# Attention over a key and value cache on one core: keys of five more pieces by plain loads and PE transposes

## The chip, the core and the metric

One core of a Trainium2 chip runs the whole program in one launch. The metric is device time in microseconds (us), the median of several executions. The engines are named as in the profile: PE (TensorE, matmuls and transposes), ACT (ScalarE), DVE (VectorE), POOL (GpSimd) and SP (SyncE, which here only issues DMAs). Each engine runs its own instructions in the order in which they are written and waits on semaphores for the others.

## The reference

```
B, Sq, D = 8, 112, 640;  H, Sk, Dh = 32, 512, 192
q = (x @ wq).reshape(B, Sq, H, Dh).transpose(0, 2, 1, 3)
scores = einsum("bhqd,bhkd->bhqk", q, k_cache) * Dh ** -0.5
p = softmax(scores)
o = einsum("bhqk,bhkd->bhqd", p, v_cache)
return o.transpose(0, 2, 1, 3).reshape(B, Sq, H * Dh) @ wo
```

All inputs and the output are bf16. The caches are 50 MB each; x is 1.1 MB, wq and wo are 7.9 MB each.

## The kernel before

**Tiles.** The 32 heads are cut into NR = 4 rounds of HU = 8 heads. A piece is one round of one batch element: 8 heads x 512 keys x 192 numbers, 1.57 MB of keys and as much of values; there are 32 pieces, in order of round, then batch. A step is half a piece (4 heads): step n belongs to piece n // 2, and there are 64 of them, S0 to S63. A group g is a round and half of the batch (4 elements), 8 in all.

**Work of PE.** `("X", c)` transposes rows of x (5 transposes). `("Q", g, lp, c)` makes 128 columns of q for a pair of heads and a group: 5 matmuls of 128x448 (line 566); ACT moves the result to `qr` (line 571). `("S", n)` makes the scores of a step: 8 full matmuls (lines 611 and 613) and 8 over 64 rows, two side by side in the two row halves of PE (lines 624 and 626). DVE then takes the minimum of the negated scores and copies them (`smax`, line 639), ACT does the exponential (line 644), DVE the reciprocal of the sum and the normalization (line 648). `("PT", n)` turns the probabilities on PE with 32 transposes over 64 or 48 rows, side by side in the two row halves (line 682); DVE and ACT move them out (line 695). `("PVt", n)` and `("PVm", n)` multiply with values (lines 715 and 726); ACT moves the result (line 736). `("O", g, m, part)` is half of a block of the output projection, 6 matmuls of 128x448 (line 748; 224 columns in group 7), which DVE adds to `accT` (lines 762 and 763). `("OF", b)` turns the output, and a DMA stores it.

**Keys.** The scores need keys with the 192 numbers of a head on partitions. For pieces 2 to 31 `load_k` (line 130) has the DMA engines transpose on the way in (`dma_start_transpose`, line 136) into one of KS = 4 buffers of `kt`. For pieces 0 and 1 (NPL = 2) `load_kn` (line 165) brings keys as they lie into a staging place `kn`: the third value buffer `vt[:, 2]` for piece 0, and wo's region for piece 1. `("K", i, u, bank, engine)` then turns one head on PE, 6 transposes of 128x128 (line 541) into one PSUM bank, and ACT or DVE moves 128x768 numbers to `kt` (line 547).

**Order.** Nothing is scheduled at run time. Four lists, ORDER_PE, ORDER_ACT, ORDER_DVE and ORDER_SP (lines 193, 270, 352 and 487), give each engine's order; a program made them beforehand. `Plan.run` emits the waits from the dependencies that each entry names. Banks 0 to 3 of PSUM hold scores; the other entries get a bank number in the list, mostly 4 to 7, and wait until that bank's last user has been moved out (`fill`, line 870).

**Loads.** All loads and stores are issued by SP, in the order of ORDER_SP; an entry that waits holds back all behind it. `("KN", i, lo, n)` are the plain key loads, `("K", i)` the transposing ones, `("V", i)` values (3 buffers, so V(i) waits for the use of V(i-3)), `("WQ", r, lp, n)` pieces of wq (round r, pairs of heads lp on; it waits for the last Q fills that read the round before), `("WO", r)` wo of a round, `("TD", n)` probabilities of five late steps, which a DMA turns in place of PE, and `("OUT", b)` stores. A Q fill of group g is moved out to one of 8 slots, so that it waits for the last score of group g-2 that read the slot.

Of the kernel before, what the change touches and what calls it, by code (L numbers as in the profile page):

```python
# [7 lines left out]
ACTF = mybir.ActivationFunctionType  # L8
# [44 lines left out]
def build_mha_kernel(nc, x, k_cache, v_cache, wq, wo, out):  # L53
    B, SQ, D = x.shape
# [3 lines left out]
    HU = 8  # L58
# [9 lines left out]
    NPL = 2  # L68
# [17 lines left out]
    with ExitStack() as es:  # L86
# [26 lines left out]
        kn = [vt[:, VS - 1], wo_flat[:, 0:HU * 768].rearrange("p (u c) -> p u c", u=HU)]  # L113
# [28 lines left out]
        def load_v(i):  # L142
            r, b = divmod(i, B)

            def emit(e):
                src = v_cache[b, r * HU:(r + 1) * HU].rearrange("u (r q) d -> r u (q d)", q=4)
                return e.dma_start(vt[:, i % VS], src)
            deps = [("PVm", 2 * (i - VS) + j, 1) for j in range(2)] if i >= VS else []
            if i == VS - 1:
                deps = [("KT", 0, u) for u in range(HU)]  # L150
            add("SP", ("V", i), deps, emit, f"mV{i % VS}", 16)
# [13 lines left out]
        def load_kn(i, lo, hi):  # L165

            def emit(e):
                return e.dma_start(kn[i][:, lo:hi, :], k_cache[i, lo:hi].rearrange("u (r q) d -> r u (q d)", q=4))
            add("SP", ("KN", i, lo, hi - lo), [], emit, f"mKN{i}_{lo}", 16)
            kn_of.update({(i, u): ("KN", i, lo, hi - lo) for u in range(lo, hi)})  # L170
# [14 lines left out]
        def load_wo(r):  # L185
# [4 lines left out]
            old = [("O", 2 * r - 1, m, 1) for m in range(DC)] if r else [("KT", 1, u) for u in range(HU)]  # L190
# [3 lines left out]
            ("X", 0, 7, "ACT"), ("X", 1, 4, "DVE"), ("K", 0, 0, 0, "DVE"), ("K", 0, 1, 2, "ACT"), ("X", 3, 3, "DVE"),  # L194
            ("X", 2, 0, "DVE"), ("K", 0, 2, 5, "ACT"), ("K", 0, 3, 6, "ACT"), ("Q", 0, 0, 1, 4), ("Q", 0, 1, 1, 0),
            ("Q", 0, 0, 2, 1), ("Q", 0, 1, 2, 3), ("Q", 0, 1, 0, 1), ("K", 0, 6, 4, "ACT"), ("Q", 0, 0, 0, 7),
            ("Q", 0, 3, 2, 2), ("S", 0), ("Q", 0, 3, 0, 6), ("Q", 0, 3, 1, 7), ("Q", 0, 2, 2, 5), ("Q", 0, 2, 0, 3),
            ("Q", 0, 2, 1, 1), ("K", 1, 3, 2, "DVE"), ("K", 0, 5, 7, "DVE"), ("K", 0, 7, 4, "ACT"),
            ("K", 1, 1, 6, "DVE"), ("K", 0, 4, 2, "DVE"), ("X", 4, 5, "ACT"), ("K", 1, 2, 7, "ACT"),
            ("X", 5, 2, "ACT"), ("X", 6, 4, "ACT"), ("K", 1, 5, 1, "DVE"), ("K", 1, 0, 3, "DVE"),  # L200
            ("K", 1, 4, 5, "ACT"), ("S", 1), ("Q", 1, 0, 1, 5), ("K", 1, 7, 6, "DVE"), ("Q", 1, 0, 2, 4),
            ("K", 1, 6, 7, "ACT"), ("S", 2), ("PT", 0, 5), ("Q", 1, 2, 0, 4), ("Q", 1, 0, 0, 7), ("Q", 1, 1, 0, 5),
            ("Q", 1, 1, 1, 7), ("Q", 1, 3, 0, 4), ("S", 3), ("PT", 1, 5), ("Q", 1, 1, 2, 7), ("PVt", 0, 4),
            ("PVt", 1, 6), ("PVm", 0), ("PVm", 1), ("S", 4), ("PT", 2, 4), ("Q", 1, 3, 2, 1), ("Q", 1, 3, 1, 7),
            ("S", 5), ("PT", 3, 5), ("PVt", 2, 4), ("PVm", 2), ("S", 6), ("PVt", 3, 4), ("PT", 4, 6), ("PVm", 3),
            ("S", 7), ("Q", 1, 2, 1, 7), ("PT", 5, 4), ("PVt", 4, 6), ("PVm", 4), ("Q", 1, 2, 2, 1), ("PT", 6, 5),
            ("S", 8), ("PVt", 5, 5), ("PVm", 5), ("Q", 2, 0, 1, 4), ("Q", 2, 0, 2, 1), ("Q", 2, 0, 0, 7), ("S", 9),
            ("PT", 7, 6), ("PVt", 6, 0), ("PVm", 6), ("Q", 2, 2, 1, 5), ("S", 10), ("PVt", 7, 4), ("Q", 2, 1, 0, 7),
            ("PVm", 7), ("PT", 8, 6), ("Q", 2, 2, 2, 4), ("S", 11), ("PT", 9, 4), ("Q", 2, 1, 1, 6), ("S", 12),
            ("PVt", 8, 4), ("PVt", 9, 6), ("PVm", 9), ("PVm", 8), ("Q", 2, 1, 2, 0), ("PT", 10, 4), ("Q", 2, 3, 2, 1),  # L210
            ("O", 0, 1, 0, 6), ("O", 0, 0, 0, 7), ("O", 0, 0, 1, 7), ("O", 0, 1, 1, 6), ("S", 13), ("PT", 11, 4),
            ("Q", 2, 2, 0, 7), ("Q", 2, 3, 1, 1), ("PVt", 10, 4), ("PVt", 11, 6), ("PVm", 11), ("PVm", 10),
            ("O", 0, 4, 0, 6), ("S", 14), ("PT", 12, 4), ("Q", 3, 0, 1, 7), ("O", 0, 2, 0, 4), ("Q", 2, 3, 0, 5),
            ("O", 0, 4, 1, 6), ("S", 15), ("PT", 13, 5), ("O", 0, 2, 1, 4), ("O", 0, 3, 0, 5), ("O", 0, 3, 1, 5),
            ("S", 16), ("PVt", 12, 6), ("PVm", 12), ("PT", 14, 4), ("PVt", 13, 0), ("PVm", 13), ("Q", 3, 1, 0, 7),
            ("Q", 3, 0, 2, 6), ("PT", 15, 4), ("S", 17), ("PVt", 14, 5), ("PVm", 14), ("Q", 3, 2, 0, 1),
            ("PVt", 15, 4), ("PVm", 15), ("S", 18), ("PT", 16, 4), ("Q", 3, 0, 0, 7), ("O", 1, 0, 0, 6), ("S", 19),
# [12 lines left out]
            ("PVt", 27, 5), ("PT", 28, 0), ("PVm", 27), ("O", 2, 2, 0, 4), ("O", 2, 2, 1, 4), ("Q", 4, 3, 0, 7),  # L230
            ("S", 31), ("PT", 29, 5), ("Q", 5, 0, 0, 4), ("O", 2, 3, 0, 6), ("O", 2, 3, 1, 6), ("S", 32),
            ("PVt", 28, 4), ("PVt", 29, 6), ("PVm", 28), ("PVm", 29), ("PT", 30, 0), ("O", 2, 4, 0, 7),
            ("O", 2, 4, 1, 7), ("S", 33), ("PT", 31, 6), ("Q", 5, 0, 2, 5), ("Q", 5, 1, 0, 4), ("Q", 5, 0, 1, 5),
            ("S", 34), ("PVt", 30, 6), ("PVt", 31, 4), ("PVm", 30), ("PVm", 31), ("PT", 32, 6), ("O", 3, 0, 0, 1),
            ("O", 3, 0, 1, 1), ("PT", 33, 4), ("S", 35), ("PVt", 32, 4), ("PVt", 33, 6), ("PVm", 33), ("PVm", 32),
            ("S", 36), ("O", 3, 2, 0, 7), ("PT", 34, 4), ("O", 3, 1, 0, 6), ("Q", 5, 1, 1, 0), ("Q", 5, 1, 2, 3),
            ("O", 3, 1, 1, 6), ("S", 37), ("Q", 5, 2, 0, 6), ("O", 3, 3, 0, 4), ("O", 3, 2, 1, 7), ("PT", 35, 5),
            ("O", 3, 3, 1, 4), ("S", 38), ("PVt", 34, 6), ("PVm", 34), ("Q", 5, 2, 1, 5), ("Q", 5, 3, 2, 0),
            ("PT", 36, 4), ("PVt", 35, 6), ("Q", 5, 2, 2, 0), ("Q", 5, 3, 0, 1), ("PVm", 35), ("Q", 5, 3, 1, 4),
            ("S", 39), ("PT", 37, 5), ("O", 3, 4, 0, 4), ("O", 3, 4, 1, 4), ("PVt", 36, 6), ("PVm", 36), ("S", 40),  # L240
            ("PT", 38, 5), ("Q", 6, 1, 0, 7), ("Q", 6, 0, 0, 0), ("Q", 6, 0, 2, 1), ("PVt", 37, 3), ("PVm", 37),
# [771 lines left out]
```

## Time and profile before

| what | us |
|---|---|
| median of 3 runs (448.17 to 450.05) | 448.45 |
| the profiled execution, its own time | 448.98 |
| span of its instructions | 447.0 |
| ACT, exponentials (line 644), 256 x 715 ns | 182.6 |
| DVE, minimum and copy of scores (line 639), 256 x 684 ns | 169.8 |
| PE, Q fills (line 566), 480 x 353 ns | 101.9 |
| PE, output projection (line 748), 480 x 341 ns | 93.5 |

The page gives busy time of each engine and its share of the span, the span in 40 slices with one digit each (9 stands for 90% or more), and groups of instructions. Matmuls are pipelined: the 353 ns of one Q matmul overlap the next, which starts about 190 ns after it, so that counts are priced by the distance of starts and not by the mean duration. A wait is shown as the engine's idle time before an instruction and what ended it.

### The profile page before, as it was taken

The page shows a single profiled execution, that of the slowest core. Times are in us where ns is not written, and L with a number is a line of the kernel's source. Part 1 is how long each engine was busy: PE and PEld are TensorE (multiplying, and loading weights), DVE is VectorE, ACT ScalarE, POOL GpSimd, SP SyncE. Part 2 cuts the span into 40 slices and gives each one's busy share as a digit, 9 for nine tenths or more (in the row PEclk, how much of TensorE's full clock was granted, in tenths as well). Part 3 has the DMA queues.
Part 4 walks back from the last instruction along what each step waited for, and adds up shares of the span by engine and source line. Part 5 has one row for each costly group of instructions (what it writes and reads, how often), then busy time and mean ns, then how long its engine had stood idle before and what let it go on. Part 6 is the DMA issues. An engine that isn't in the chain of part 4 may idle for free.

```text
span 447.0 us, 14859 instructions
## 1 busy us (share of the span) xinstructions
PE 423.9 (95%) x6229; PEld 295.9 (66%) x6229; DVE 353.5 (79%) x1142; ACT 332.9 (74%) x753; POOL 0.7 (0%) x6
## 2 busy tenths in 40 slices
PE   8999788999999999999999999999999999999996
PEld 5566555666666666776676666666676757665886
DVE  1368897876989877888898877898789968899862
ACT  2689888885768778797679748788668676974784
POOL 0000000000000000000000000000000000000000
PEclk9999999999999999999999999999999999999999
DMA  8999999999999999999999999999999999999782
GB/s 273 373 349 201 211 239 325 364 314 240 251 303 223 244 351 366 231 325 307 210 321 292 240 251 254 360 328 246 321 240 245 236 268 367 301 204 235 212 225 64
DMA packets 247858, 121.93 MB, mean 273 GB/s; under 512 B 195440, under 2 KB 247792, under 8 KB 247792
## 3 DMA queue, kind: packets, MB, share of 16 engines
q1 hardware_dynamic: 247792, 120.99, 109.8%
q8 instruction: 49, 0.80, 0.8%
q14 instruction: 17, 0.14, 0.1%
HBM read 70.35 MB, written 1.15 MB: 160 GB/s over the span
## 4 chain that ended last, share of the span: by engine, by line
PE 70%; DVE 15%; ACT 7%; DMA 3%; issue 3%; SPq 0%; DVEq 0%; ACTq 0%
PE ps L566 17%; PE ps L748 15%; DVE s_sb L639 9%; PE ps L726 8%; PE ps L624 6%; PE ps L611 6%; PE ps L613 5%; PE ps L715 5%; PE ps L682 5%; ACT p_sb L644 3%; DVE p_sb L648 2%; DVE pT_sb L695 2%; DMA wq_sb<-in_wq_dram 2%; DMA wq_sb<-p_sb 2%; ACT oT_sb L736 1%
## 5 line engine op out<-in xcount | busy, mean ns | idle before, releaser
L644 ACT ACTIVATE p_sb<-s_sb,nmx 112x512 bf16<-112x512 f32 x256 | 182.6, 715 | 46.6 <-DVE s_sb L639 30.8
L639 DVE TENSOR_SCALAR_CACHE_REDUCE s_sb<-ps 112x512 f32<-112x512 f32 x256 | 169.8, 684 | 36.7 <-PE ps L626 18.8
L566 PE MATMUL ps<-xT_sb,wq_sb 128*128 128x448 bf16 x480 | 101.9, 353 | 4.0 <-DVE s_sb L639 2.5
L748 PE MATMUL ps<-oT_sb,wo_sb 128*128 128x448 bf16 (+1 forms) x480 | 93.5, 341 | 0.4 <-ACT qr L571 0.4
L648 DVE TENSOR_SCALAR p_sb<-p_sb,rinv 112x512 bf16<-112x512 bf16 x256 | 80.3, 347 | 1.3
L566 PEld LDWEIGHTS ps<-xT_sb,wq_sb 128*128 128x128 bf16 x480 | 42.8, 98 | 43.4 <-DVE s_sb L639 4.2
L748 PEld LDWEIGHTS ps<-oT_sb,wo_sb 128*128 128x128 bf16 x480 | 44.0, 98 | 36.7 <-ACT pT_sb L695 0.9
L736 ACT ACTIVATE oT_sb<-ps 128x672 bf16<-128x672 f32 x64 | 45.8, 724 | 25.6 <-PE ps L726 25.1
L571 ACT ACTIVATE qr<-ps 128x448 bf16<-128x448 f32 x96 | 49.7, 536 | 19.0 <-PE ps L566 18.5
L695 ACT ACTIVATE pT_sb<-ps 128x768 bf16<-128x768 bf16 x59 | 47.2, 800 | 11.5 <-PE ps L682 10.5
L726 PE MATMUL ps<-pT_sb,vt 128*128 128x112 bf16 x944 | 54.5, 213 | 0.0
L726 PEld LDWEIGHTS ps<-pT_sb,vt 128*128 128x128 bf16 x944 | 47.5, 98 | 4.0
L644 ACT ACTIVATION_READ_ACCUMULATOR p_sb<-s_sb,nmx 112x1 f32 x256 | 48.8, 191 | 0.0
L695 DVE COPY pT_sb<-ps 128x1024 bf16<-128x1024 bf16 x59 | 40.4, 685 | 6.7 <-PE ps L682 5.7
L682 PEld LDWEIGHTS ps<-ident,p_sb 64*128 64x128 bf16 (+1 forms) x1888 | 32.3, 94 | 15.4 <-DVE p_sb L648 6.6
L682 PE MATMUL ps<-ident,p_sb 64*128 64x64 bf16 (+1 forms) x1888 | 37.6, 185 | 4.5 <-DVE p_sb L648 1.2
L611 PE MATMUL ps<-kt,qr 128*112 128x256 bf16 x128 | 36.2, 283 | 3.8 <-DVE s_sb L639 2.2
L715 PE MATMUL ps<-pT_sb,vt 128*64 128x112 bf16 x944 | 32.5, 215 | 4.6 <-ACT pT_sb L695 2.6
L715 PEld LDWEIGHTS ps<-pT_sb,vt 128*64 128x64 bf16 x944 | 25.4, 109 | 15.1 <-ACT pT_sb L695 4.8
L613 PE MATMUL ps<-kt,qh 128*112 128x256 bf16 x128 | 34.9, 273 | 0.0
L613 PE MATMUL ps<-kt,qr 128*112 128x256 bf16 x128 | 34.9, 273 | 0.0
L611 PE MATMUL ps<-kt,qh 128*112 128x256 bf16 x128 | 34.9, 273 | 0.0
(60 smaller groups left out, 451.3 us busy)
## 6 DMA issues: line engine op xcount, KB each, us to landing
vt<-in_v_cache_dram SPq DMA_DIRECT2D x32, 1536.0 KB, 10.2
wo_sb<-in_wo_dram SPq DMA_DIRECT2D x4, 1920.0 KB, 13.6
wq_sb<-in_wq_dram SPq DMA_DIRECT2D x14, 480.0 KB, 7.3
vt<-in_k_cache_dram SPq DMA_DIRECT2D x2, 768.0 KB, 7.4
wo_sb<-in_k_cache_dram SPq DMA_DIRECT2D x1, 1536.0 KB, 12.7
out_dram<-xT_sb SPq DMA_DIRECT2D x8, 140.0 KB, 3.1
wq_sb<-in_wq_dram SPq DMA_DIRECT2D x1, 960.0 KB, 10.3
kt<-in_x_dram SPq DMA_DIRECT2D x2, 320.0 KB, 4.5
```

What stands on the lines that cost most here:

```text
L566: mm = e.matmul(ps[:, bank, 0:SG], wq_sb[:, dc, c0:c0 + 128], xT_sb[:, dc, bh * SG:(bh + 1) * SG], start=(dc == 0), stop=(dc == DC - 1))
L611: e.matmul(ps[0:SQ, 2 * j, hs], ev, ktb[:, :, 0, cs(i)], start=(h == 0), stop=False, skip_group_check=True)
L613: mm = e.matmul(ps[0:SQ, 2 * j + 1, hs], od, ktb[:, :, 2, cs(i)], start=(h == 0), stop=False, skip_group_check=True)
L639: return e.tensor_scalar(s_sb[:, a, :].rearrange("p (e c) -> p e c", e=2), ps[0:SQ, 2 * j:2 * j + 2, h * 256:(h + 1) * 256], -scale, None, ...
L644: return e.activation(p_sb[:, k, :], s_sb[:, a, :], ACTF.Exp, bias=nmx[:, k:k + 1], scale=-1.0, accum_out=rsum[:, k:k + 1])
L648: return e.tensor_scalar(p_sb[:, k, :], p_sb[:, k, :], rinv[:, k:k + 1], None, op0=ALU.mult)
L682: ends.append(e.transpose(psb[:, bank + t, i * w:(i + 1) * w], p_sb[lo:hi, (4 * n + k) % 8, q * 128:(q + 1) * 128], ident[lo:hi, lo:hi]))
L695: return e.activation(dst, src, ACTF.Copy) if j == 0 else e.tensor_copy(dst, src)
L715: mm = e.matmul(ps[64 * h:64 * h + 64, b0 + j, SQ:2 * SQ], vtb[:, h0 + 2 * j + h, d0:d0 + 64], pT(j, h, q), start=(q == 0), stop=(q == 3))
L726: mm = e.matmul(ps[:, b0 + j, 2 * h * SQ:(2 * h + 1) * SQ], vtb[:, h0 + 2 * j + h, d0:d0 + 128], pT(j, h, q), start=(q == 0), stop=(q == 3))
L736: return e.activation(dst.rearrange("p (j c) s -> p j c s", j=2), ps[:, b0:b0 + 2, 0:3 * SQ].rearrange("p j (c s) -> p j c s", c=3), ACTF. ...
L748: mm = e.matmul(ps[:, bank_of["O", g, m, 0], 0:nc_], wo_sb[:, k, m * 128:(m + 1) * 128], oT_sb[:, g % 2, k, 0:nc_], start=(k == 0), stop=( ...
```

## The change

Keys of pieces 2 to 6 no longer come by transposing DMAs. NPL goes from 2 to 7: their keys are loaded as they lie, into staging places that alternate between wo's region (pieces 1, 3, 5) and a part of `accT`'s region behind that of x (pieces 2, 4, 6). A load of keys waits until the piece two before it has been turned; the first load of wo waits until pieces 1, 3 and 5 are turned; the first sums into `accT` wait for pieces 2, 4 and 6.

The turning of keys, now for 7 pieces, is done for two heads at a time: 12 pairs of transposes over 64 rows, one in each row half of PE, into two PSUM banks, and two moves of 128x768 numbers, each on ACT or DVE. From piece 4 on a move also waits until the scores that last read the `kt` buffer are done. Before there were 16 entries of one head with one move each (8 on ACT, 8 on DVE); now there are 28 entries of two heads with two moves each (25 on ACT, 31 on DVE). All four lists are new, over the whole length of the kernel.

```diff
-    NPL = 2
+    NPL = 7
...
-        kn = [vt[:, VS - 1], wo_flat[:, 0:HU * 768].rearrange("p (u c) -> p u c", u=HU)]
+        kn = [vt[:, VS - 1]]
+        for i in range(1, NPL):
+            flat = wo_flat[:, 0:HU * 768] if i % 2 else acc_flat[:, 3 * D:3 * D + HU * 768]
+            kn.append(flat.rearrange("p (u c) -> p u c", u=HU))
...
-                deps = [("KT", 0, u) for u in range(HU)]
+                deps = [("KT", 0, p) for p in range(LP)]
...
-            add("SP", ("KN", i, lo, hi - lo), [], emit, f"mKN{i}_{lo}", 16)
+            old = [("KT", i - 2, p) for p in range(lo // 2, hi // 2)] if i > 2 else []
+            add("SP", ("KN", i, lo, hi - lo), old, emit, f"mKN{i}_{lo}", 16)
...
-            old = [("O", 2 * r - 1, m, 1) for m in range(DC)] if r else [("KT", 1, u) for u in range(HU)]
+            old = [("O", 2 * r - 1, m, 1) for m in range(DC)] if r else [("KT", i, p) for i in range(1, NPL, 2) for p in range(LP)]
...
-        def k_transposes(i, u, bank, eng):
-            def emit(e):
-                for c in range(6):
-                    mm = e.transpose(psb[:, bank, c * 128:(c + 1) * 128], kn[i][:, u, c * 128:(c + 1) * 128], ident[:, :])
-                return mm
...
-            add("PE", ("KT", i, u), [kn_of[i, u]], emit)
-            add(eng, ("evK", i, u), [("KT", i, u)], evac)
+        def k_transposes(i, p, bank, engs):
+            def emit(e):
+                for x in range(12):
+                    c, u = divmod(x, 2)
+                    ends = [e.transpose(psb[:, bank + t, x * 64:(x + 1) * 64],
+                                        kn[i][64 * t:64 * t + 64, 2 * p + u, c * 128:(c + 1) * 128],
+                                        ident[64 * t:64 * t + 64, 64 * t:64 * t + 64]) for t in range(2)]
+                return tuple(ends)
+
+            add("PE", ("KT", i, p), [kn_of[i, 2 * p], kn_of[i, 2 * p + 1]], emit, ("PE", "PE2"))
+            old = [("St", 2 * (i - KS) + 1, 3)] if i >= KS else [("XT", x) for x in range(4)] if i == KS - 1 else []
+            for t in range(2):
+                def evac(e, t=t):
+                    dst = kt[:, i % KS].rearrange("p a m (u t s) -> p (a m) u t s", t=2, s=64)[:, :, 2 * p:2 * p + 2, t, :]
+                    src = psb[:, bank + t, 0:768].rearrange("p (c u s) -> p c u s", c=6, u=2)
+                    return e.activation(dst, src, ACTF.Copy) if engs[t] == "ACT" else e.tensor_copy(dst, src)
+                add(engs[t], ("evK", i, p, t), [("KT", i, p)] + old, evac)
...
-                    ([("evK", n // 2, 4 * qd + i) for i in range(4)] if n // 2 < NPL else [("K", n // 2)]), emit)
+                    ([("evK", n // 2, 2 * qd + i, t) for i in range(2) for t in range(2)] if n // 2 < NPL else [("K", n // 2)]), emit)
...
-            deps = [("O", g, m, 1)] + ([("oacc", g - 2, m)] if r else [("XT", c) for c in range(4, B * SQ // 128)])
+            deps = [("O", g, m, 1)] + ([("oacc", g - 2, m)] if r else
+                                         [("XT", c) for c in range(4, B * SQ // 128)] +
+                                         [("KT", i, p) for i in range(2, NPL, 2) for p in range(LP)])
```

SP's list, its first part before and after:

```diff
-            ("X", 0), ("KN", 0, 0, 4), ("X", 1), ("WQ", 0, 0, 1), ("WQ", 0, 1, 1), ("KN", 0, 4, 4), ("WQ", 0, 2, 2),
-            ("KN", 1, 0, 8), ("X", 2), ("V", 0), ("V", 1), ("V", 2), ("K", 2), ("K", 3), ("K", 4), ("K", 5), ("K", 6),
-            ("WQ", 1, 0, 1), ("WQ", 1, 2, 1), ("V", 3), ("WQ", 1, 1, 1), ("V", 5), ("V", 4), ("WQ", 1, 3, 1),
-            ("WO", 0), ("V", 6), ("K", 7), ("K", 9), ("K", 8), ("V", 7), ("V", 8), ("K", 11), ("K", 10), ("K", 12),
+            ("X", 0), ("X", 1), ("WQ", 0, 1, 1), ("WQ", 0, 0, 1), ("KN", 0, 0, 4), ("X", 2), ("WQ", 0, 2, 2),
+            ("KN", 0, 4, 4), ("KN", 1, 0, 8), ("KN", 2, 0, 8), ("V", 2), ("V", 0), ("WQ", 1, 0, 1), ("KN", 3, 0, 8),
+            ("KN", 4, 0, 8), ("V", 1), ("V", 3), ("WQ", 1, 2, 1), ("WQ", 1, 1, 1), ("KN", 5, 0, 8), ("WQ", 1, 3, 1),
+            ("KN", 6, 0, 8), ("V", 4), ("K", 7), ("K", 8), ("WO", 0), ("V", 6), ("V", 5), ("V", 7), ("K", 10),
```

PE's list from S5 to S13, after (K has the piece, the pair of heads, the bank and the two engines):

```
("S", 5), ("K", 3, 1, 6, "ACT", "DVE"), ("PT", 3, 4), ("PVt", 2, 6), ("K", 3, 2, 4, "ACT", "DVE"), ("PVm", 2),
("S", 6), ("K", 4, 1, 4, ...), ("K", 4, 2, 6, ...), ("K", 4, 0, 4, ...), ("K", 4, 3, 0, ...), ("Q", 2, 1, 0, 7),
("PT", 4, 4), ("Q", 2, 0, 0, 6), ("PVt", 3, 0), ("PVm", 3), ("K", 5, 1, 5, ...), ("S", 7), ("PT", 5, 4), ("PVt", 4, 6),
("PVm", 4), ("Q", 2, 0, 2, 5), ("S", 8), ("K", 5, 3, 4, ...), ("PT", 6, 6), ("Q", 2, 0, 1, 5), ("K", 5, 0, 0, ...),
("Q", 2, 2, 1, 4), ("K", 5, 2, 6, ...), ("S", 9), ("PVt", 5, 4), ("PVm", 5), ("K", 6, 2, 6, ...), ("PT", 7, 0),
("Q", 2, 2, 2, 6), ("Q", 2, 1, 1, 7), ("S", 10), ("PVt", 6, 6), ("PVm", 6), ("K", 6, 0, 4, ...), ("K", 6, 3, 0, ...),
("PT", 8, 6), ("Q", 2, 3, 1, 1), ("Q", 2, 2, 0, 0), ("PVt", 7, 5), ("PVm", 7), ("Q", 2, 3, 0, 1), ("K", 6, 1, 4, ...),
("PT", 9, 6), ("S", 11), ("PVt", 8, 4), ("PVt", 9, 6), ("PVm", 9), ("PVm", 8), ("S", 12), ("PT", 10, 5),
("O", 0, 0, 0, 4), ("Q", 2, 1, 2, 6), ("Q", 2, 3, 2, 7), ("O", 0, 0, 1, 4), ("S", 13)
```

## The prediction

> **What bounds the kernel now.** I read the totals and slices of the page first, then the busy time stage by stage, then SP's queue, and last the rows that price the parts of the change. A stage here runs from the first score matmul of one step to that of another (S0 starts at 17.3 us, S5 at 51.7, S9 at 75.5, S13 at 101.8, S63 at 427.8, read from the timeline's L611 rows).
>
> ```profile
> span 447.0 us, 14859 instructions
> ...
> PE 423.9 (95%) x6229; PEld 295.9 (66%) x6229; DVE 353.5 (79%) x1142; ACT 332.9 (74%) x753; POOL 0.7 (0%) x6
> ...
> DMA  8999999999999999999999999999999999999782
> GB/s 273 373 349 201 211 239 325 364 314 240 251 303 223 244 351 366 231 325 307 210 321 292 240 251 254 360 328 246 321 240 245 236 268 367 301 204 235 212 225 64
> ```
>
> Two resources are near full: PE at 95% and the DMA queue, whose slices stay at nine tenths until about 402 us. The GB/s row tells the two kinds of transfer apart: 349 to 373 in the early slices, where plain loads run, 201 and 211 in the fourth and fifth, where keys come by DMA transposes.
>
> ```profile
> core 0: us, PE busy (x) PEld busy (x) DVE busy (x) ACT busy (x) POOL busy (x), PEclk, DMA share, GB/s
> 17.30:51.70 34.40, 31.91 (x397) 21.79 (x397) 25.68 (x82) 28.50 (x65) 0.00 (x0) 1.00 1.20 266
> 51.70:75.50 23.80, 19.77 (x346) 13.91 (x347) 21.06 (x71) 19.51 (x46) 0.00 (x0) 1.00 1.18 275
> 75.50:101.80 26.30, 24.56 (x375) 16.92 (x375) 20.97 (x69) 21.63 (x51) 0.00 (x0) 1.00 1.11 338
> 101.80:427.80 326.00, 318.23 (x4692) 220.60 (x4691) 274.66 (x888) 244.83 (x561) 0.00 (x0) 1.00 1.14 274
> 427.80:447.00 19.20, 14.76 (x325) 13.46 (x321) 8.39 (x28) 10.81 (x21) 0.00 (x0) 0.99 0.45 142
> ```
>
> From S13 to S63 PE is busy 97.6% of the time. From S0 to S13 it is 76.2 of 84.5 us (90%); the worst part is S5 to S9, where DVE (21.1 of 23.8) leads and PE idles 4.0 us. The granted clock is 1.00 nearly throughout and plays no part.
>
> ```profile
> 25.88 41.57 SPq L136 DMA_TRANSPOSE kt<-in_k_cache_dram  x5
> 67.50 1.14 SPq L179 DMA_DIRECT2D wq_sb<-in_wq_dram  x2
> 68.69 0.53 SPq L147 DMA_DIRECT2D vt<-in_v_cache_dram  x1
> ```
>
> SP's timeline shows why fillers are missing there: the transposes of pieces 2 to 6 hold SP from 25.9 to 67.5 us, and wq of round 1 is issued only then. Its first piece lands 4.8 us after issue (the view of line 179 in that window), at 72.3; the first Q of group 2 starts at 72.5. V of piece 3 lands 9.3 us after issue, at 78.0, and is used at 78.4.
>
> **The change, part by part.**
>
> ```profile
> 26.66 1.17 PE L541 MATMUL ps<-ident,wo_sb 128*128 128x128 bf16 x18
> ...
> 34.48 0.52 PEld L682 LDWEIGHTS ps<-ident,p_sb 64*128 64x128 bf16 x32
> ```
> ```profile
> PEld ps L624 <- issue: 11.4, 64, 0.2
> ```
> ```profile
> L547 ACT ACTIVATE kt<-ps 128x768 bf16<-128x768 bf16 x8 | 6.3, 806 | 0.0
> L547 DVE COPY kt<-ps 128x768 bf16<-128x768 bf16 x8 | 4.2, 552 | 8.8 <-PE ps L541 8.8
> ```
>
> *PE, key transposes.* Old form: 18 matmuls in 1.17 us less the last one's tail, 56 ns apart, so 0.335 us a head, 16 heads: 5.4 us. The new form (64-row matmuls in two row halves) is that of the probability transposes: 32 loads in 0.52 us, less the last one's 0.09, is 15 further pairs in 0.43: 29 ns a pair. A pair of heads has 12 pairs of matmuls: 0.35 us; 28 pairs of heads: 9.7 us. Net +4.4 us.
>
> *PE, changes of tiling.* At 64 of 64 steps PE's loads wait 0.18 us on "issue" where the 128-row score matmuls hand over to the 64-row ones; start to start this is 0.20 us instead of the 0.11 inside a run, so a change costs 0.095 us. Counting changes between full, 64-row and 64-column matmuls in the two lists: 45 against 64 up to S13 (+1.8 us), 216 against 190 behind it (-2.5 us). In all PE's work grows by 3.7 us.
>
> *PE, work moved.* Up to S13 the new list holds three more Q fills (5 matmuls, 0.95 us each) and two fewer O halves (1.14 us each): with keys and changes of tiling +6.7 us there. From S13 to S63 the Q and O come back (-0.5 us), the changes give -2.5, and four O halves of group 7 (0.575 us each) go behind S63: -5.3, and -5.0 when every entry is summed at its own rows. Behind S63: +2.0.
>
> *ACT and DVE.* The key evacuations grow from 8 to 25 on ACT and 8 to 31 on DVE, all ahead of S13. Back to back one takes 0.70 us on ACT (chain: 1.41 for two), 0.47 on DVE: +11.9 and +10.8 us.
>
> *DMA and SP.* The last four of the five transposes leave SP 27.6 us apart in sum, 6.9 each; a plain 1.57 MB at the 366 GB/s of 17 to 33 us takes 4.3. Five make the queue 13 us lighter, and wq of round 1 moves from behind the transposes to among the key loads. I credit no gain for this by itself: it shows only as a better filled PE, below. The Trainium skill, Advanced Engine Details and Errata, X-Bar Transpose (TRN2), says transposing DMAs are as fast as plain ones; 6.9 against 4.3 us here says otherwise. By that rule the queue would not get lighter and the faster rival below would lose its support; the sum would stay.
>
> *New waits on SP, which issues in order.* wq of lane pair 0, round 1, waits for Q(1,0,*), which come after S1; behind it queue the keys of 3 and 4 and V of 1, used from S3 on. Keys of 5 wait for piece 3's last turn (after S5) and hold wq(1,3), keys of 6, V4 and K7. PE has 7.6 us of listed work before it wants them; alone they need 4.3 us plus 2 (an output's landing), under load 12.7 (keys of piece 1): 0 to 5 us late, I take 0 since only two 480 KB pieces are ahead. wo now waits for pieces 1, 3 and 5 and stands behind K8, which waits for S9: about 7 us of issue and 15.6 to land (wo's first load, before) against 21.6 us until its first use: 0 to 2 us late, I take 0. Both ends stay in the range.
>
> *Sum.* Stage loads of after are those of the stage table plus what the two lists add, at these prices and those of the timeline's rows. S5 to S9, as an example: ACT 19.5 + 10 key evacuations x 0.70, one evacuation of Q and one of PV fewer and one of probabilities more (-0.4) = 26.1; PE 19.8 + 10 x 0.35 + 0.4 for changes of tiling - 1.2 for one PV fewer = 22.5; DVE 21.1 + 10 x 0.47 - 0.67 for one copy of q fewer = 25.1. S0 to S5 likewise: PE 33.3, ACT 31.6, DVE 28.7. S9 to S13: PE 26.2, ACT 24.0, DVE 23.2. The busiest engine's loads add to 33.3 + 26.1 + 26.2 = 85.6; before, they add to 31.9 + 21.1 + 24.6 = 77.6 in 84.5 us, 92%. With less waiting for loads the share should rise, but three engines with nearly equal loads that hand over to each other will not reach the 97.6% that PE reaches alone later. I take the middle, 94.8%: 90.3 us, +5.8 (bounds +1.1 at 100%, +8.5 at 92%, +12.1 if ACT's additions hide nowhere). S0 itself: by the lists PE has 1.0 us more ahead of it, and x and wq come with 0.79 MB of keys fewer ahead of them, 2.1 us at 366 GB/s: I take 0 (-1 to +1). S13 to S63: -5.0 if PE sets the pace, 0 if the hand-over between DVE and ACT does; PE is the busiest by far (318 against 275), so -4.0. Behind S63: PE idles 4.4 of 19.2 us and part of the 2.0 falls there: +0.7 (0 to +2). Sum: +5.8 - 4.0 + 0.7 = +2.5 us. The profiled execution took 448.98 us for a span of 447.0, 0.5 above the median 448.45; from that median: **451.0 us**.
>
> **Rivals.**
> *The lighter queue pays (faster).* The slack of 0.2 and 0.4 us at wq and V3 says that loads set the pace from S5 to S12. If all of the early idle time was theirs, the early stage runs at its busiest engine's load (+1.1), the later one at PE's (-5.1), and the tail hides: -4.0, 444.4 us. For it: PE idles 4.0 us just where wq is late. Against it: DVE leads there, and DVE and ACT get the most new work. It decides once the early stage grows by less than 2 us.
> *Evacuation becomes the bound (slower).* ACT's 12.1 us come on top: +12.1 - 4.0 + 0.7 = +8.8, 457.3 us. For it: S5 to S9 makes ACT the busiest (26.1), with work that exps wait behind. Against it: ACT idled 18% of S0 to S13. The Trainium skill, TensorEngine Tiling (Array Packing), PSUM Bottleneck, has it that tiling speeds TensorE but not the emptying of PSUM; the trace agrees in kind, 0.35 us to turn a pair of heads against 0.70 + 0.47 to empty it.
> *The halves don't run side by side.* Then a pair of heads takes 24 x 29 ns = 0.70 us, +9.8 us of PE: 460.8 us at most. The probability transposes speak against it.
>
> **How the numbers follow.** Forecast 0.41 (its own range 447 to 455, four parts in ten of it under 450.7), faster rival 0.31, evacuation 0.20, not side by side 0.08. A measurement here can't tell less than 0.5% (446.2 to 450.7) from no change. Faster by more: the rival but for its upper edge, 0.28. Within: that edge and 0.17 of the forecast, 0.20. Slower by more: the rest of the forecast and the last two, 0.52. The range leaves one in ten on each side: 443.5 to 457.5.
>
> **What would show it.** S13 at about 107.6 us (102.9 for the faster rival, 113.9 for evacuation); ACT busier than PE between S5 and S9; 0.35 us for a pair of heads at the new transposes; S13 to S63 in about 322 us; no wait of Q on wq and none of O on wo. A first O that waits for wo, or turns of pieces 5 and 6 that wait for their loads, would make the forecast wrong upwards; PE over 95% busy from S5 to S9 would make it wrong downwards.

## The result, and the profile after

The changed kernel takes 445.86 us (median of 19 runs, 443.96 to 448.78), the kernel before 448.37 (19 runs, 447.41 to 451.85) on the same chip: ratio 0.9938, 95% interval 0.9919 to 0.9958. It is 0.6% faster, where 2.5 us slower had been forecast. Medians, here and below, are over all runs of a kernel, but ratios and their intervals leave out runs more than 1.5% above that kernel's fastest. The profiled execution of the changed kernel took 446.26 us for a span of 444.4.

First the page after: span, busy time of PE, DVE and ACT, and four rows of the 40 slices.

```profile
span 444.4 us, 16108 instructions
...
PE 425.1 (96%) x6805; PEld 304.5 (69%) x6805; DVE 363.2 (82%) x1165; ACT 344.4 (78%) x770; POOL 0.7 (0%) x6
...
PEclk9999999999999999999999999999999999989999
DMA  8999999998999999999999999999999999999952
GB/s 278 373 337 323 347 299 285 226 342 276 232 289 317 215 270 270 365 247 288 238 223 324 301 236 267 360 370 234 234 266 313 256 267 371 234 173 242 237 176 80
```

The fourth and fifth slices move 323 and 347 GB/s where before they moved 201 and 211: plain loads run there now. PEclk has one 8 near the end, of which more below. Now the busy time stage by stage; the cuts are the starts of S0, S5, S9, S13, S25, S41, S55 and S63 in this trace.

```profile
core 0: us, PE busy (x) PEld busy (x) DVE busy (x) ACT busy (x) POOL busy (x), PEclk, DMA share, GB/s
17.50:52.80 35.30, 33.23 (x609) 22.63 (x609) 29.00 (x88) 31.79 (x69) 0.00 (x0) 1.00 1.00 345
52.80:77.40 24.60, 22.70 (x555) 16.80 (x553) 23.56 (x75) 24.44 (x52) 0.00 (x0) 1.00 1.03 292
77.40:106.90 29.50, 26.64 (x500) 19.11 (x497) 24.39 (x81) 26.06 (x59) 0.00 (x0) 1.00 1.12 305
106.90:184.50 77.60, 77.60 (x1155) 54.32 (x1154) 66.52 (x210) 58.04 (x135) 0.00 (x0) 1.00 1.13 266
184.50:284.20 99.70, 98.29 (x1512) 69.77 (x1511) 87.80 (x288) 80.25 (x185) 0.00 (x0) 1.00 1.17 277
284.20:372.80 88.60, 88.13 (x1332) 61.76 (x1331) 75.24 (x245) 68.23 (x155) 0.00 (x0) 1.00 1.15 288
372.80:423.10 50.30, 47.92 (x673) 35.82 (x672) 43.28 (x143) 37.14 (x87) 0.00 (x0) 0.97 1.06 236
423.10:444.40 21.30, 16.45 (x346) 15.42 (x344) 9.05 (x31) 11.44 (x23) 0.00 (x0) 1.00 0.39 122
```

The first column behind each stretch is its length. From S5 to S9 ACT is busy 24.44 of 24.60 us, so it leads there. From S13 to S25 PE is busy all 77.60 us. The same stages, with the forecast beside what was measured (us, both from the profiled executions):

| part | before | after | forecast | measured |
|---|---|---|---|---|
| up to S0 | 17.3 | 17.5 | 0 | +0.2 |
| S0 to S13 | 84.5 | 89.4 | +5.8 | +4.9 |
| S13 to S63 | 326.0 | 316.2 | -4.0 | -9.8 |
| behind S63 | 19.2 | 21.3 | +0.7 | +2.1 |
| span | 447.0 | 444.4 | +2.5 | -2.6 |

So nearly the whole error lies between S13 and S63. What PE's weight loads waited for between S13 and S63, before (first fence) and after (second); the columns are total us, times, longest:

```profile
PEld ps L682 <- DVE p_sb L648: 5.1, 13, 0.6
PEld ps L715 <- ACT pT_sb L695: 3.0, 5, 1.2
```
```profile
PEld ps L706 <- DVE p_sb L672: 1.2, 5, 0.4
PEld ps L739 <- ACT pT_sb L719: 0.8, 2, 0.5
```

These are the hand-overs of the softmax: the probability transposes wait for DVE's normalised rows, the PV matmuls for ACT's moved transposes. The two waits shrink from 8.1 to 2.0 us in sum. Over all rows of this view that name DVE or ACT the sum is 25.7 us before and 12.1 after. Most of it passes while PE still works on earlier matmuls: of PE's own idle time, waits for DVE and ACT made 5.9 us before and make 0.5 after. That is a change of order only, since none of the softmax work was added or removed.

### The profile page after: what moved, and what is told of

Same layout as the page of the kernel before. It is cut to its first block, busy times and chain, and to the rows that moved or that the text cites. A ratio compares the mean times of both kernels' runs of the same rounds, so it can differ in the third digit from the quotient of the medians.

```text
span 444.4 us, 16108 instructions
## 1 busy us (share of the span) xinstructions
PE 425.1 (96%) x6805; PEld 304.5 (69%) x6805; DVE 363.2 (82%) x1165; ACT 344.4 (78%) x770; POOL 0.7 (0%) x6
## 4 chain that ended last, share of the span: by engine, by line
PE 84%; DVE 5%; ACT 5%; DMA 4%; issue 2%; SPq 0%; ACTq 0%
PE ps L772 19%; PE ps L590 18%; PE ps L750 12%; PE ps L648 7%; PE ps L739 7%; PE ps L635 6%; PE ps L637 6%; PE ps L706 5%; DVE s_sb L663 3%; DMA wo_sb<-in_k_cache_dram 2%; PE ps L561 2%; ACT p_sb L668 2%; DMA wq_sb<-in_wq_dram 2%; ACT qr L595 1%; DVE p_sb L672 1%
## 5 line engine op out<-in xcount | busy, mean ns | idle before, releaser
L672 DVE TENSOR_SCALAR p_sb<-p_sb,rinv 112x512 bf16<-112x512 bf16 x256 | 81.3, 347 | 1.5
L595 ACT ACTIVATE qr<-ps 128x448 bf16<-128x448 f32 x96 | 49.6, 539 | 12.7 <-PE ps L590 12.1
L750 PE MATMUL ps<-pT_sb,vt 128*128 128x112 bf16 x944 | 55.8, 215 | 2.0 <-issue 2.0
L706 PEld LDWEIGHTS ps<-ident,p_sb 64*128 64x128 bf16 (+1 forms) x1888 | 33.3, 94 | 5.8 <-DVE p_sb L672 2.0
L650 PE MATMUL ps<-kt,qh 64*112 64x256 bf16 x128 | 34.1, 291 | 0.1
L648 PE MATMUL ps<-kt,qr 64*112 64x256 bf16 x128 | 34.0, 291 | 0.0
```

What stands on the lines that cost most here:

```text
L595: return e.activation(qr[:, q_slot(g, lp), c, :], ps[:, bank, 0:SG], ACTF.Copy)
L648: m1 = e.matmul(ps[0:SQ, 2 * j, hs], ev, ktb[0:64, :, 1, cs(i)], start=False, stop=True, skip_group_check=True)
L672: return e.tensor_scalar(p_sb[:, k, :], p_sb[:, k, :], rinv[:, k:k + 1], None, op0=ALU.mult)
L706: ends.append(e.transpose(psb[:, bank + t, i * w:(i + 1) * w], p_sb[lo:hi, (4 * n + k) % 8, q * 128:(q + 1) * 128], ident[lo:hi, lo:hi]))
L750: mm = e.matmul(ps[:, b0 + j, 2 * h * SQ:(2 * h + 1) * SQ], vtb[:, h0 + 2 * j + h, d0:d0 + 128], pT(j, h, q), start=(q == 0), stop=(q == 3))
```

## The experiments

All numbers below are from one table, so that they can be compared: time (median), ratio to the kernel before with its interval, then from the profiled execution the start of S13 and the length of four stages (start of the first score matmul of one step to that of another).

| run | us | ratio, 95% interval | S13 at | 13-25 | 25-41 | 41-55 | 55-63 |
|---|---|---|---|---|---|---|---|
| before | 448.37 | 1 | 101.8 | 82.6 | 102.2 | 92.2 | 48.9 |
| after | 445.86 | 0.994 [0.992, 0.996] | 106.9 | 77.6 | 99.7 | 88.6 | 50.3 |
| new_early_old_late | 458.41 | 1.020 [1.015, 1.024] | 109.7 | 84.0 | 102.9 | 92.2 | 48.7 |
| old_early_new_late | 450.07 | 1.002 [0.998, 1.005] | 105.3 | 80.2 | 99.4 | 95.6 | 50.7 |
| keys_2_to_6_by_dma | 458.10 | 1.018 [1.013, 1.022] | 111.9 | 77.6 | 98.5 | 100.1 | 51.2 |
| keys_5_6_by_dma | 449.63 | 0.999 [0.996, 1.002] | 106.0 | 77.9 | 99.2 | 95.3 | 48.3 |
| after_v19_first | 449.89 | 0.995 [0.991, 1.000] | 107.3 | 77.6 | 98.6 | 96.7 | 48.0 |
| keys_5_6_by_dma_v19_first | 452.25 | 1.006 [1.003, 1.010] | 107.1 | 79.1 | 98.6 | 98.5 | 46.5 |
| old_early_new_late_v19_first | 452.44 | 1.008 [1.005, 1.011] | 105.4 | 78.8 | 100.0 | 97.3 | 47.4 |
| after_v19_late | 455.30 | 1.012 [1.006, 1.017] | 107.0 | 77.6 | 98.5 | 97.9 | 48.5 |
| after_loads_by_use | 457.92 | 1.019 [1.013, 1.024] | 110.2 | 77.6 | 98.4 | 95.3 | 56.6 |
| keys_5_6_by_dma_loads_by_use | 454.16 | 1.012 [1.008, 1.016] | 107.0 | 77.6 | 99.6 | 90.2 | 57.6 |
| old_early_new_late_loads_by_use | 453.82 | 1.010 [1.006, 1.014] | 105.1 | 80.1 | 99.2 | 94.2 | 53.2 |
| old_early_new_late_loads_moved | 454.76 | 1.008 [1.005, 1.012] | 105.5 | 78.5 | 103.3 | 92.3 | 52.4 |
| after_loads_moved | 452.88 | 1.002 [0.998, 1.006] | 107.7 | 77.6 | 98.5 | 91.0 | 56.2 |
| old_early_new_late_18_21_cut | 445.04 | 0.987 [0.981, 0.992] | 105.4 | 79.2 | 100.0 | 88.6 | 51.6 |
| before_18_21_cut | 448.71 | 0.999 [0.997, 1.001] | 101.2 | 82.6 | 102.3 | 92.1 | 49.3 |
| after_18_21_cut | 444.27 | 0.990 [0.986, 0.993] | 107.8 | 77.6 | 98.4 | 88.5 | 50.5 |

Ratios are to runs of the kernel before on the same chip, so they need not equal the quotient of two medians of this table.

### Which half of the lists, and the queue

The change brings two things at once to the steps behind S13: another order of the work, and a DMA queue that has some 13 us less to move (five pieces, 6.8 us by transpose against 4.2 plain). Theory L: the new later order gives the gain. Theory Q: it takes the lighter queue. Two hybrids have one half of each kernel. The edit, for all four lists:

```diff
 # new_early_old_late: the changed kernel's entries up to S13, then what is left of before's lists in before's order
 # old_early_new_late: before's entries (NPL = 2) up to S13, then what is left of the changed kernel's
+order = first[:cut] + [e for e in second if e not in first[:cut]]
```

> The changed kernel up to S13, then the order of the kernel before for everything that is left. Theory Q: the old later order also gains from loads that are 13 us further ahead, S13 to S63 falls from 326 to about 320 and the span is 446 to 448, ratio about 1.00. Theory L: S13 to S63 stays at 325 to 326, S13 is at 107, and the span is 451 to 453, ratio about 1.01.

> The kernel before up to S13 (its lists, its transposing loads for keys 2 to 6), then the changed kernel's order for everything that is left on all engines; the first halves of two O blocks keep the old banks. If the later order alone gives the gain (theory L), S13 comes at 102 us, S13 to S63 takes 316 us as in the changed kernel, and the span is about 439 us, ratio about 0.98. If the later gain needs the lighter DMA queue (theory Q), loads come late, S13 to S63 takes 322 to 326 us and the span is 445 to 449, ratio 0.995 to 1.005, with PE waits on loads or S steps that start within 3 us of their keys' landing.

S13 comes at 109.7 us and 105.3, later than in the kernel whose early half each has: two halves of O (first hybrid) and three Q fills (second) that the other list has ahead of S13 now stand ahead of it as well.

The old later order with the light queue (new_early_old_late), from S13 on:

```profile
109.70:193.70 84.00, 78.93 (x1170) 53.86 (x1168) 65.96 (x213) 59.11 (x136) 0.00 (x0) 0.98 0.93 224
193.70:296.60 102.90, 101.15 (x1489) 69.45 (x1489) 87.21 (x281) 79.42 (x183) 0.00 (x0) 1.00 1.13 278
296.60:388.80 92.20, 89.80 (x1364) 62.09 (x1364) 77.29 (x247) 68.91 (x156) 0.00 (x0) 1.00 1.15 277
```

84.0, 102.9 and 92.2 us, against 82.6, 102.2 and 92.2 before: no gain. But only the start of the first stage had its loads further ahead: V9 lands 9.1 us before its use, against 3.0 in the kernel before, V10 3.4 against 2.9 and V19 4.3 against 4.0. With the old order of SP's list the lead is gone by V10, so for the later stages this hybrid does not test a lighter queue; before_18_21_cut, below, does. The new later order with the heavy queue gains in S13 to S25 and S25 to S41 (80.2 and 99.4) but loses in S41 to S55: 95.6, slower than before. (Its 80.2 instead of 77.6 hold a 2.2 us wait of PE for `accT` just behind the seam of the two lists, and a stretch of half clock after it.) What PE waited for there (old_early_new_late, S41 to S55):

```profile
PE ps L718 <- DMA vt<-in_v_cache_dram: 3.7, 1, 3.7
PE ps L569 <- DMA wq_sb<-in_wq_dram: 0.8, 1, 0.8
```

One load of values, V19, is late by 3.7 us. So L holds for two stages and Q for the third, which neither had said.

### Keys given back to the DMA

Next, the changed kernel with its own order, and the keys of five or two pieces transposed by the DMA again, their loads standing where the plain ones stood and their turns taken out of PE's list:

```diff
-    NPL = 7
+    NPL = 2      # keys_2_to_6_by_dma
+    NPL = 5      # keys_5_6_by_dma
-            ... ("KN", 5, 0, 8), ("WQ", 1, 3, 1), ("KN", 6, 0, 8), ...
+            ... ("K", 5), ("WQ", 1, 3, 1), ("K", 6), ...
```

> The changed kernel with all its lists, but keys of pieces 2 to 6 come by transposing DMAs again, at the places of the plain loads, and their 20 turns and 40 evacuations are left out of the lists; pieces 0 and 1 are still turned in two row halves. Theory L: PE has about 7.5 us and ACT 11 us less to do and the order is kept, so the span falls to 438 to 441, ratio 0.98 to 0.985. Theory Q: the queue is 13 us heavier, Q of round 1, values or wo come late before S13 and keys and values run within 3 us of their use after it: the span is 446 or more, ratio 0.995 to 1.01.

> The changed kernel, but keys of pieces 5 and 6 by transposing DMAs at the places of their plain loads, and their 8 turns and 16 evacuations left out. PE has 3 us less before S13 and ACT 5.6 us; the queue is 5 us heavier. Theory L: S13 comes 3 us earlier and the span is 441 to 442, ratio 0.987. Theory Q: loads after S13 have 20 to 40 us to spare in the changed kernel, 5 us less hurts nothing until wq, V19 and wo at 280 us, which have none: the gain of 3 us is kept before S13 and mostly given back at 280 us, 442 to 445.

S13 to S25 and S25 to S41 keep their gain in both (77.6 and 98.5, 77.9 and 99.2), with either queue. 5.0 us of what keys_2_to_6_by_dma loses against the changed kernel are lost before S13. S41 to S55 grows with what the queue carries: 88.6, 95.3, 100.1 us for 0, 2 and 5 pieces given back. PE stands there before V19 again: 3.8 us with two pieces, 3.2 with five, and the latter has 1.5 us before wq besides, and 1.9 us with no releaser in the profile.

### One late transfer, or the whole queue

In the changed kernel V19 lands 0.40 us before its first use, wo of the next round 0.16 us before its own. If only that one transfer stands wrong in SP's list, moving it should mend all. The edit of SP's list, in three kernels, and its opposite in a fourth:

```diff
 # *_v19_first
-    ("K", 21), ("K", 20), ("K", 22), ("WQ", 3, 0, 1), ("WQ", 3, 1, 1), ("V", 20), ("WQ", 3, 2, 1), ("V", 19),
-    ("WQ", 3, 3, 1), ("WO", 2),
+    ("K", 21), ("V", 19), ("K", 20), ("WQ", 3, 0, 1), ("K", 22), ("WQ", 3, 1, 1), ("WQ", 3, 2, 1),
+    ("WQ", 3, 3, 1), ("WO", 2), ("V", 20),
 # after_v19_late
-    ("V", 19), ("WQ", 3, 3, 1), ("WO", 2),
+    ("WQ", 3, 3, 1), ("WO", 2), ("V", 19),
```

> The changed kernel with V19 four to seven places earlier in SP's list (behind K21), and WQ(3,0) ahead of K22, V20 behind WO2. Everything else is the changed kernel. V19 had 0.40 us to spare there. Theory 'one transfer' (what the heavier queues lost in steps 41 to 55 hangs on when V19 lands): V19's margin grows to over 10 us, steps 41 to 55 stay at 88 to 89 us since nothing waited for it, and the time stays within 2 us of the changed kernel's 445.9 (ratio to before 0.990 to 0.998). Theory 'whole queue' (the later order needs a light queue as such): the same time here, since the queue's load is the same.

> keys_5_6_by_dma with the same edit of SP's list. Theory 'one transfer': steps 41 to 55 come down from 95.3 us to 88 to 90, no stretch of half clock follows at 290 us, and the whole is 5 to 7 us shorter than keys_5_6_by_dma: 440 to 444 us, ratio to before 0.982 to 0.990, so faster than both kernels. Theory 'whole queue': another transfer (WQ(3,3) or WO2, which had 0.84 and 0.16 us to spare in the changed kernel) is late in V19's place, steps 41 to 55 stay at 94 us or more, and the ratio stays at 0.997 to 1.0.

> old_early_new_late (before's lists up to step 13, every key transposed by the DMA; the changed kernel's lists behind) with the same edit of SP's list. Theory 'one transfer': steps 41 to 55 come down from 95.6 us to 88 to 90 and the whole by 5 to 7 us, to 443 to 445 us (ratio 0.985 to 0.992): then the whole gain of the change is to be had without one key turned by PE beyond the old two. Theory 'whole queue': with the full old load the stage stays at 94 us or more and the ratio at 0.998 to 1.004.

> The changed kernel with V19 moved two places back, behind WO2, and nothing else; the light queue stays. V19 had 0.40 us to spare, and WQ(3,3) and WO2 take 1.5 and 5.4 us on the queue: it lands some 6 to 7 us later. Theory 'one transfer': PE stands some 4 to 6 us ahead of PVt38, half a clock follows for 3 to 7 us, and steps 41 to 55 take 95 to 100 us as with the heavier queues; the whole is 6 to 11 us longer than the changed kernel (452 to 457). Theory 'whole queue': the light queue makes up for most of it; under 3 us lost.

The fourth did what was said: PE stood 8.0 us before V19, even longer than the 4 to 6 expected, and the stage took 97.9 us. The other three missed in this stage (96.7, 98.5 and 97.3 us). V19 was in time, but another load of values was not (after_v19_first, S41 to S55):

```profile
PE ps L740 <- DMA vt<-in_v_cache_dram: 4.7, 1, 4.7
PE ps L636 <- DVE p_sb L673: 1.4, 1, 1.4
```

The 4.7 us stand before the PV matmuls of step 46, that is before V23, at 341.6 us. The 12 runs of this kernel spread from 443.2 to 455.2 us (the profiled one took 450.4), and its ratio, 0.995, is that of the changed kernel, so it alone decides nothing. But in the other two PE waits for V23 as well, 3.5 and 2.4 us, and their ratios are 1.006 and 1.008. 'One transfer' falls. Two more orders of the loads were worked out from the landing times of the runs so far, the first from K11 to K31, close to the order of use, the second from K14 to K28:

```diff
 # *_loads_by_use, about the same place
+    ("K", 20), ("V", 18), ("V", 19), ("WQ", 3, 0, 1), ("K", 21), ("K", 22), ("WQ", 3, 2, 1), ("WQ", 3, 3, 1), ("WO", 2),
 # *_loads_moved
+    ("K", 20), ("V", 17), ("WQ", 3, 0, 1), ("V", 18), ("K", 21), ("K", 22), ("V", 19), ("WQ", 3, 2, 1), ("WQ", 3, 3, 1),
```

> The changed kernel with the loads from K11 on put in another order in SP's list (between V8 and TD57), nearly that of their use, so that loads which had 20 to 30 us to spare stand behind those that had under 1 us; PE, ACT and DVE lists as they are. Worked out from the landings of the changed kernel, its smallest margin between 110 and 390 us is 4 us instead of 0.2. Theory 'order of loads': no gap of PE at a V, steps 41 to 55 take 87.5 to 89 us in every run, and the time is at or a little under the changed kernel's: 442 to 446 us, ratio to before 0.984 to 0.994, with less spread than after_v19_first (443 to 455). Theory 'whole queue': the queue has no reserve, any change of order makes some load late, steps 41 to 55 take 93 us or more and the ratio is 0.995 to 1.005.

> old_early_new_late (old lists and old key loads up to step 13) with the same order of the loads from K11 on. Theory 'order of loads': steps 13 to 25 at 75 to 78 us, 41 to 55 at 87.5 to 89.5 us, the time 440 to 445 us (ratio 0.980 to 0.991): the plain loads and PE's added turns would not be needed for the gain. Theory 'whole queue': with the old load of the queue some load is late in every order, 93 us or more in steps 41 to 55, ratio 0.998 to 1.008.

> The changed kernel with the same second order of the loads K14 to K28. Theory 'order': no margin under 3 us up to 370 us, steps 41 to 55 at 87.5 to 89 us, time 442 to 446 (ratio 0.984 to 0.994). Theory 'load': with the light queue it holds as well, so the same here; if this one too takes 93 us or more in steps 41 to 55, the model of the queue is wrong and the order that the changed kernel has fits by details that it lacks.

> old_early_new_late with all its bytes and a second order of the loads, K14 to K28 only, the tail as in the changed kernel, worked out with the landing times that all runs so far show (a key behind another load 7.0 us): its smallest margin is 3.4 us if the queue is 4 us late, under 0 if it is 8 us late. Theory 'order': steps 41 to 55 at 88 to 90.5 us, 443 to 446 us (ratio 0.986 to 0.994). Theory 'load': some load is late again, 93 us or more, ratio 0.997 to 1.01.

All missed, on the changed kernel too, as did keys_5_6_by_dma_loads_by_use. After_loads_by_use shows how (S41 to S63, PE's waits):

```profile
PE ps L636 <- DVE s_sb L664: 7.4, 2, 7.1
PE ps L591 <- DMA wq_sb<-in_wq_dram: 4.9, 1, 4.9
```

PE waits 4.9 us for wq, which stands behind K21 and K22. The 7.1 us from 411 us on are put down to DVE, but ACT stood 9.7 us, up to 416.8, for the probability transposes that the DMA makes at the end (the timeline's row of line 669, released by "DMA wq_sb<-p_sb"): they stand behind K30 and K31, which landed 19 and 17 us later than in the changed kernel. So these runs say that my picture of the queue was not good enough to find a better order, not that there is none. That stays open. No run that loads every key beat the changed kernel.

### The load alone

The last set leaves the order of the loads as it is and takes bytes away: seven eighths of the keys K18 and K21, due around 250 and 290 us, are not loaded, and steps 36, 37, 42 and 43 use old keys for the other seven heads. At 6.8 us a piece that is 12 us, about what the change takes off the queue.

```diff
-                return e.dma_start_transpose(kt[:, i % KS].rearrange("p a m c -> p (a m) c"), src)
+                n = 128 if i in (18, 21) else HU * 128
+                return e.dma_start_transpose(kt[:, i % KS].rearrange("p a m c -> p (a m) c")[:, :, 0:n], src[0:n])
```

> old_early_new_late (order of SP's list untouched) with seven eighths of the keys K18 and K21 left out: only their first 128 rows are loaded, so steps 36, 37, 42 and 43 use old keys for the other units. The queue has 2 x 7/8 x 6.8 = 12 us less to move, between 225 and 265 us, as much as the change takes off it early. Theory 'load' (the new order of steps 41 to 55 needs a queue that is ahead): steps 41 to 55 come down from 95.6 us to 88 to 90, the clock there stays whole, and the time comes down by 5 to 7 us from 450.1 to 443 to 445 (ratio to before 0.985 to 0.992). Theory 'order' (it is the place of V19, V23 and their like in SP's list that makes the stall, at any load): the stage stays at 94 us or more, ratio 0.997 or more.

> The kernel before with seven eighths of the keys K18 and K21 left out, as in old_early_new_late_18_21_cut: the queue has 12 us less to move between 225 and 265 us, the old later order is untouched. If the old order has nothing to gain from a queue that is ahead (as new_early_old_late showed with the plain loads), steps 41 to 55 stay at 92 us and the ratio to before is 0.995 to 1.003. If a lighter queue pays under any order: 41 to 55 under 90 us, ratio under 0.992.

> The changed kernel with seven eighths of the keys K18 and K21 left out in the same way. V19 had 0.4 us to spare in its profile and WO2 0.2. If the changed kernel's queue is just light enough, steps 41 to 55 stay at 88 to 89 us and the time is 0 to 2 us under the changed kernel's 445.9 (ratio to before 0.988 to 0.996). If its later steps still pay for late loads in most executions, 3 us or more are gained: ratio under 0.987.

The stage from S41 to S55 in old_early_new_late, whole (first fence) and with the cut (second):

```profile
284.90:380.50 95.60, 90.60 (x1331) 63.35 (x1330) 75.21 (x245) 68.27 (x155) 0.00 (x0) 0.96 1.12 272
```
```profile
284.60:373.10 88.50, 88.04 (x1331) 61.74 (x1330) 75.11 (x245) 68.10 (x155) 0.00 (x0) 1.00 1.15 277
```

Same order, same PE work, 12 us less for the queue just ahead: 7.1 us go, the clock is back from 0.96 to 1.00, and the whole is 1.3% faster than before. The same cut gives the kernel before nothing (ratio 0.999, 92.1 us) and the changed kernel nothing in this stage (88.5). In the kernel before the cut did put loads further ahead here (V19 8.8 us before its use instead of 4.0), so the old order had a lighter queue and made nothing of it. This settles the third stage: the new order shortens S41 to S55 by 3.6 us only if the queue is ahead, and the plain loads put it there. In the changed kernel the queue is light enough. The small margins of V19 and wo there (0.40 and 0.16 us) do not say by how much: with 12 us less to move they are 0.50 and 0.30. They come from a wait of SP. Just ahead of V19 in its list stands a piece of wq that waits for the last Q fills of the round before, and SP waits for PE, in the changed kernel (first line) and with the cut (second), from 270 to 280 us:

```profile
SPq L183 <- PE ps L590: 4.9, 1, 4.9
```
```profile
SPq L184 <- PE ps L591: 8.1, 1, 8.1
```

## Why the prediction was wrong

**The step that failed** is "S13 to S63: -5.0 if PE sets the pace, 0 if the hand-over between DVE and ACT does; PE is the busiest by far (318 against 275), so -4.0". It measured -9.8. The work inside it may stand (summed from the lists and rows; no run measures it alone), but the bound does not: I took the old order's waits as given and let only the work change. PE busy fell by 6.3 us (318.2 to 311.9), although half clock cost 1.7 (last section), so some 3 us more than the 5.0 of work; its idle time fell by 3.5 (7.8 to 4.3). 97.6% busy had looked like no room, but 5.9 of the 7.8 idle us were waits for DVE and ACT, and 0.5 are left. That the 3 us of busy time were such waits too, too short to show as idle, fits the weight loads' waits (25.7 to 12.1) but is argued, not shown. By stage: S13 to S25 -5.0 and S25 to S41 -2.5, from the order and what work stands where, with the heavy queue as with the light one; S41 to S55 -3.6, from the order and the lighter queue together; S55 to S63 +1.4, from the clock (below): keys_5_6_by_dma, with the same lists there and a clock of 1.00, takes 48.3 us, 0.6 less than before.

**"I credit no gain for this by itself: it shows only as a better filled PE"**, of the 13 us by which the queue gets lighter: half right. Under the old order a lighter queue gave nothing. Under the new one it is worth 7 us in S41 to S55 (95.6 against 88.6), more than 200 us after the loads that it saves. I looked for its effect only where wq of round 1 was late.

**S0 to S13, +5.8**: right; +4.9. The loads of the busiest engine measured 33.23, 24.44 and 26.64 us, in sum 84.3 of 89.4 us, 94.3%, where 85.6 and 94.8% were taken. ACT led from S5 to S9 as said (24.4, worked out as 26.1). The turn of a pair of heads: these two rows of the timeline have 24 and 48 matmuls at line 561.

```profile
59.88 0.52 PE L561 MATMUL ps<-ident,accT 64*128 64x64 bf16 x24
...
60.81 0.89 PE L561 MATMUL ps<-ident,accT 64*128 64x64 bf16 x48 [0.40 <-ACT kt L572]
```

The second row has one more pair of heads and takes 0.37 us more. Worked out were 0.35, and 0.70 if the halves did not run side by side, so that rival falls.

**The waits on SP**: wo was in time by 6.7 us and the keys of 5 by 1.6, both taken as 0. A wait that I had not priced was there, the keys of piece 3:

```profile
PEld ps L561 <- DMA wo_sb<-in_k_cache_dram: 1.5, 1, 1.5
```

**Behind S63, +0.7**: nearly right, though +2.1 was measured. In the 14 other runs with this end of the lists the part takes 20.1 to 20.6 us, mostly 20.1 or 20.2, so +0.9. The rest is one late store: PE begins its last transposes 16.3 us behind S63 in the changed kernel and in after_18_21_cut alike, but then SP waits for the last store to land, first line the changed kernel, second that run.

```profile
SPq L991 <- DMA out_dram<-xT_sb: 3.0, 1, 3.0
```
```profile
SPq L992 <- DMA out_dram<-xT_sb: 1.7, 1, 1.7
```

**A reading that was off**: the DMA slices of the kernel before stay at nine tenths until about 413 us, not 402. No term hangs on it.

**The rivals.** "The lighter queue pays" gave 444.4, near the measured 445.86, for the wrong reason: it had S13 at 102.9, and S13 came at 106.9. What it lacked early came late. "Evacuation becomes the bound" (S13 at 113.9) did not happen.

## What to carry to other kernels

A new order for a whole list is not priced by summing the work that it moves: what the old order lost in hand-overs is up for change too, so the wait view over the same stage is the second half of the bound (here 5.9 us of PE's idle time that I left out). A transfer that is saved early can be cashed in 200 us later, at a load with a small margin between landing and use. List these margins for every load before saying that a lighter queue gives nothing, and look at what sets each of them, the queue or a wait of SP. In this queue, nine tenths full, each of the three new orders of the loads made another load late.

## What the runs showed of the hardware

Short gaps of PE cost a second time through the granted clock. In the changed kernel PE stood for 1.96 us in the middle of the PV matmuls of step 54, waiting for nothing that the profile shows. The timeline, and the windows of 2 us around it:

```profile
386.42 0.86 PE L750 MATMUL ps<-pT_sb,vt 128*128 128x112 bf16 x14
...
389.24 0.27 PE L750 MATMUL ps<-pT_sb,vt 128*128 128x112 bf16 x2 [1.96 <-issue]
```
```profile
386.00:388.00 2.00, 1.28 (x30) 1.04 (x29) 1.96 (x7) 2.00 (x5) 0.00 (x0) 1.00 1.71 204
388.00:390.00 2.00, 0.76 (x18) 0.68 (x18) 1.96 (x9) 0.72 (x3) 0.00 (x0) 0.90 0.82 180
390.00:392.00 2.00, 2.00 (x26) 1.85 (x21) 0.33 (x1) 0.34 (x2) 0.00 (x0) 0.50 1.25 282
392.00:394.00 2.00, 2.00 (x33) 1.81 (x33) 0.11 (x1) 2.00 (x5) 0.00 (x0) 0.75 1.30 294
```

The clock is at 0.50 from 389.6 us for 3.41 us, and 16 PV matmuls take 1.67 us there instead of 0.96. At half speed PE loses some 1.7 us: with the gap 3.7 us, more than the stage's +1.4. Over all 18 profiles, between 20 and 426 us, PE had 11 gaps of 1.3 to 1.7 us that stood alone, and none was followed by half clock; of 20 gaps from 1.7 to 2.4 us, 14 were; of 20 longer ones, 19. Once it came without a single such gap: in after_v19_first at 83.1 us, after shorter ones that add up to 1.7 us in 3.1. The half clock mostly lasted 3.41 us, sometimes twice and once three times that. That is why a V19 late by 3.7 us cost old_early_new_late 7 us: 3.7 of standing, 6.83 us at half clock, in 5.4 of which PE had work, which are 2.7 more, and the 0.8 before wq. The Trainium skill, TensorE: Matmul & The Clock Gate, Part 1: The HAM clock gate, has the clock fall after a window of about 3.4 us without work, the windows running free; the length of the slow stretches agrees, but here gaps of 1.76 us were enough at times. What makes PE stand inside a run of like matmuls with all its inputs there was not found. It is not mere chance: after_18_21_cut and after_v19_late, with the same list for PE, stand before the same matmul of step 54, for 2.23 and 1.83 us. Other runs have such stands of 1 to 2 us at other places.
